# Both SwiGLU stages in written order: transposes by the DMA crossbar, large weight loads in pieces, the forward loop's setup beside the first projection

## The chip, the cores and the metric

The kernel runs on one core of one Trainium2 chip. The metric is the device time of one launch in microseconds (us), the median of several runs. Names used: PE is TensorE (matmuls), DVE VectorE, ACT ScalarE, POOL GpSimd, SP SyncE, which issues transfers and does no arithmetic. A transfer can be issued by SP, ACT or POOL; each is a queue that works in order.

## The reference, cut to what matters

```python
xn = layernorm(x)                      # x: 2048 x 640, bf16
s  = A(xn, mem0, Wq, Wk, Wv, Wo)       # attention over 64 segments of 32 tokens, 8 memory rows handed on
g  = silu(B(xn, w1, w3, w2))           # B: (silu(xn @ w1) * (xn @ w3)) @ w2, inner width 1728
out = x + s * g
# outputs: out, and the gradients of x, mem0, Wq, Wk, Wv, Wo, w1, w3, w2 for a given grad_out
```

A has 32 heads of width 128. Its segments depend on each other only through the 8 memory rows, so the forward pass has a chain of 64 steps, and so has the backward pass. B, the SwiGLU branch, has no such chain: its forward and its backward pass are rows of matmuls.

## The kernel before

The program is a sequence of stages on the one core:

1. `phase1_ln` normalizes 16 tiles of 128 rows, writes the rows (`XN`) and, transposed by PE, the columns (`XNT`) to memory.
2. `phase2_Bfwd` is the SwiGLU forward pass, in four blocks of 512 tokens. For each of 14 chunks of the inner width it forms gate and up product (`pg`, `pu`, lines 1631 and 1634, five matmuls each), the activation `sl` and its gradient factor `ds`, stores both (`SLT`, `DUT`), and keeps the hidden values `hBT`. Then, for each of the four row tiles of the block, it multiplies by w2 (`pz`, 28 matmuls), forms the gate (`GB`), its gradient factor (`DZ`) and the gated gradient (`GS`), and lets PE turn `gs` and `hBT` (lines 1676 and 1683) for storing `GST` and `HB` in the other layout.
3. `phase3_Afwd` begins with the first projection: v, k and q of the first 672 tokens (`b0pb`, line 385), 240 matmuls each. Then it clears its tiles, loads the memory and the first k rows (`kr`), turns them into `kT` (line 562), and runs the forward chain of 64 steps. The "ride" of a step is the part of the inputs of later tokens that is projected along with the memory rows; it is loaded from `XNT`, in the backward chain from `GST`.
4. `phase3b_out` and `phase4_Abwd`: outputs, and the backward chain, whose prologue loads two blocks `gx` (line 763) and the turned WqT.
5. `phase6_Awgrads`, `phase6b_gWo`: the weight gradients of A. `hr`, the rows of the chain's inputs (3 MB), is loaded in it; in the second, `late` loads what B's backward pass needs (`hb_all`, `w2T`).
6. `phase5_Bbwd_ln`: B's backward pass. The gradient `gz` is turned by PE (`gzp`); w2's gradient (`w2a`); then in eight blocks of 256 tokens the gradient at the hidden values (`pghb`, line 1763, 14 chunks of five matmuls), times `du` and `sl` read back (`ggT`, `guT`); the gradient of the rows (`pgxb`, line 1776, 56 matmuls a row tile) with the backward layernorm after it; and PE's turn of `ggT` and `guT` (`ptt`, line 1783) into rows. Last the gradients of w1 and w3 (`wa`, 640 matmuls), the second half from `gutok`, which was stored (`GU`) and is read back.

`turned_load` (line 272) is a transfer that transposes on its way through the DMA crossbar, issued on SP. `k.copy` (lines 90 and 92) is a copy on DVE or ACT. A stage's instructions are put in order by a planner with costs of its own, except where the stage ends with `in_order`, which chains the instructions of every engine in the order in which they are written:

```python
def in_order(k, start):
    ...
    for ins in tc.nc.cur_bb.bb.instructions[start:]:
        p = last.get(ins.engine)
        if p is not None:
            tc.add_manual_dep(ins, p.name, ...)
```

The chains, `phase3b_out` and the weight gradients of A have it. The layernorm, both SwiGLU stages and the first projection don't: the planner orders them, and can put their loads and instructions early, among those of the stage before.

Of the kernel before, what the change touches and what calls it, by code (L numbers as in the profile page):

```python
# [40 lines left out]
class K:  # L41
# [55 lines left out]
    def setup_consts(self):  # L97
# [9 lines left out]
        self.mean_all = const.tile([P, self.NT], F32, name="mean_all")  # L107
# [44 lines left out]
    def setup_dram(self):  # L152
# [7 lines left out]
        self.XNT = mk("XNT", (D, S))  # L160
        self.SLT = mk("SLT", (F, S))
        self.DUT = mk("DUT", (F, S))
        self.HB = mk("HB", (S, F))
# [3 lines left out]
        self.GST = mk("GST", (D, S))  # L167
# [191 lines left out]

def phase3_Afwd(k, W4, Wv, Wk_):  # L360
# [4 lines left out]

    with tc.tile_pool(name="b0", bufs=1) as io, tc.tile_pool(name="b0s", bufs=3) as stp, \
            tc.tile_pool(name="b0p", bufs=4, space=bass.MemoryType.PSUM) as ps:
        xs = io.tile([P, DC, k.NB0], BF16, name="b0x")
        nc.sync.dma_start(xs[:], k.XNT[:, 0:k.NB0].rearrange("(dc p) t -> p dc t", p=P))
        wq = k.A_Wq.rearrange("(dc p) h e -> p dc (h e)", p=P)  # L370
        wo = k.A_Wo.rearrange("h e d -> e h d")
        fetch = [(Wq[:, dc], wq[:, dc]) for dc in range(DC)] + [(Wo[:, h:h + 8], wo[:, h:h + 8]) for h in range(0, H, 8)]
        n = 0
        for wi, (W, dst) in enumerate(((Wv, k.QVX[:, 1]), (Wk_, k.KX[:, :]), (Wq, k.QVX[:, 0]))):
            for x0 in range(0, k.NB0, 112):
                for cg in range(4):
                    if n % 3 == 0 and n > 5 and fetch:
                        nc.scalar.dma_start(*fetch.pop(0))
                    n += 1
                    st = stp.tile([112, 1024], BF16, name="b0st", tag="b0st")  # L380
                    for b in range(2):
                        c0 = cg * 1024 + b * 512
                        pb = ps.tile([112, 512], F32, name="b0pb", tag="b0pb")
                        for dc in range(DC):
                            nc.tensor.matmul(pb[:], xs[:, dc, x0:x0 + 112], W[:, dc, c0:c0 + 512],
                                             start=(dc == 0), stop=(dc == DC - 1))
                        k.copy(st[:, b * 512:(b + 1) * 512], pb[:], eng='vs'[b])
                    nc.sync.dma_start(dst[x0:x0 + 112, cg * 1024:(cg + 1) * 1024], st[:])
        assert not fetch

    with tc.tile_pool(name="ast", bufs=1) as st, tc.tile_pool(name="achain", bufs=1) as ch, \
            tc.tile_pool(name="afill", bufs=1) as fl, \
            tc.tile_pool(name="aps", bufs=1, space=bass.MemoryType.PSUM) as ps, \
            tc.tile_pool(name="apm", bufs=1, space=bass.MemoryType.PSUM) as psm:
# [8 lines left out]
        for i, tt in enumerate(kTs + hxs + qTs + xPs + PTs + [oTm, vt]):  # L403
            (nc.gpsimd, nc.vector)[i % 2].memset(tt[:], 0.0)
        bA, bB, bC = [psm.tile([P, 512], F32, name=f"bank{i}") for i in range(3)]
        pm = bA
        with nc.allow_non_contiguous_dma(reason="tiny mem0 transpose load"):
            for dc in range(DC):
                nc.sync.dma_start(hxs[0][:, dc, 0:8], k.mem0[:, dc * P:(dc + 1) * P].rearrange("m p -> p m"))
            nc.sync.dma_start(k.m_rows(k.HRO, 0), k.mem0)  # L410
# [3 lines left out]
        def ride_ld(t):  # L414
            x0 = k.NB0 + 24 * t
            b, sub = t // 4, t % 4
            if sub == 0 and x0 < S:
                w = min(96, S - x0)
                rt = ch.tile([P, DC, 96], BF16, name="ride", tag="ride")
                nc.sync.dma_start(rt[:, :, 0:w], k.XNT[:, x0:x0 + w].rearrange("(dc p) s -> p dc s", p=P))  # L420
                rides[b] = (rt, w)
# [241 lines left out]
        load_v(0)  # L663
        ride_ld(0)
        ride(0)
        for qd in range(8):
            ld_k(0, qd)
            kprep(0, qd)
# [89 lines left out]
    return Wo  # L758


def gx_ld(k, xs, x0, eng):
    w = min(P, k.S - x0)
    eng.dma_start(xs[:, :, 0:w], k.GST[:, x0:x0 + w].rearrange("(dc p) t -> p dc t", p=P))
# [13 lines left out]
def phase3b_out(k, Wo, W0, W4):  # L777
# [12 lines left out]
    with tc.tile_pool(name="oio", bufs=1) as io, tc.tile_pool(name="oac", bufs=1, space=bass.MemoryType.PSUM) as pa, \  # L790
# [59 lines left out]
        def gox_ld(x0):  # L850
            xs = io.tile([P, DC, P], BF16, name="g0x", tag="g0x", bufs=2)
            gx_ld(k, xs, x0, nc.scalar)
            st["gx", x0] = xs
# [59 lines left out]
def phase4_Abwd(k, out2, WoT, WvT, WkT, WqT, later):  # L913
# [3 lines left out]
    with tc.tile_pool(name="gst", bufs=1) as st, tc.tile_pool(name="gchain", bufs=1) as ch, \  # L917
# [26 lines left out]
        def ride_ld(t):  # L944
# [3 lines left out]
            if sub == 3:  # L948
                rt = ch.tile([P, DC, 96], BF16, name="gride", tag="gride")
                nc.sync.dma_start(rt[:], k.GST[:, 96 * b:96 * b + 96].rearrange("(dc p) s -> p dc s", p=P))  # L950
                rides[b] = rt
# [278 lines left out]
        def gox(x0, cg, b):  # L1230
            if cg == 0 and b == 0:
                uu["gx"] = ch.tile([P, DC, P], BF16, name="gx0", tag="xp", bufs=1)
                gx_ld(k, uu["gx"], x0, nc.gpsimd)
# [31 lines left out]
def phase6_Awgrads(k, X, out0, out3, out4, out5):  # L1265
# [12 lines left out]
    with tc.tile_pool(name="h6i", bufs=3) as io, tc.tile_pool(name="h6", bufs=1) as hp, \  # L1278
# [173 lines left out]
        for qd in range(8):  # L1452
            u0 = NTL * qd
            for p in range(NTL):
# [16 lines left out]
                if u == 6:  # L1471
                    nc.sync.dma_start(hr[0:120], k.HRO[0:120 * NF, :].rearrange("(t p) d -> p t d", p=120))
# [25 lines left out]
def phase6b_gWo(k, gow, orr0, out6, gz, late):  # L1498
# [4 lines left out]
    with tc.tile_pool(name="o6", bufs=1) as hp, tc.tile_pool(name="o6i", bufs=2) as io, \  # L1503
# [28 lines left out]
        for qd in range(8):  # L1532
            orr = orrs[qd]
            for jp in range(2):
# [4 lines left out]
                if qd > 1 and late:  # L1539
                    out_, in_ = late.pop(0)  # L1540
                    if in_ is k.w2:
                        turned_load(k, out_, in_)
                    else:
                        nc.scalar.dma_start(out_, in_)
# [8 lines left out]
                for j in range(2):  # L1553
# [4 lines left out]
                    nc.sync.dma_start(out6f[hh * P:(hh + 1) * P, :], ot[:])  # L1558
# [5 lines left out]
def phase1_ln(k: K):  # L1564
    nc, tc = k.nc, k.tc
    D, DC, NT = k.D, k.DC, k.NT
    with tc.tile_pool(name="ln_io", bufs=3) as io, tc.tile_pool(name="ln_sm", bufs=4) as sm, \
            tc.tile_pool(name="ln_ps", bufs=2, space=bass.MemoryType.PSUM) as ps:
        half = D // 2
        assert half <= nc.vector.BN_STATS_FMAX  # L1570
        for tt in range(NT):
            xt = io.tile([P, D], BF16, name="xt", tag="xt")
            k.dma(xt[:], k.A_x[tt * P:(tt + 1) * P, :])
            stats = sm.tile([P, 2, nc.vector.BN_STATS_DIM], F32, name="stats", tag="stats")
            xv = xt[:].rearrange("p (a b) -> p a b", a=2)
            nc.vector.bn_stats(stats[:, 0, :], xv[:, 0, :])
            nc.vector.bn_stats(stats[:, 1, :], xv[:, 1, :])
            mv = sm.tile([P, nc.vector.BN_AGGR_DIM], F32, name="mv", tag="mv")
            nc.vector.bn_aggr(mv[:], stats[:])
            rs = k.rstd_all[:, tt:tt + 1]  # L1580
            nc.scalar.activation(rs, mv[:, 1:2], ACT.Sqrt, bias=k.eps_t[:], scale=1.0)
            nc.vector.reciprocal(rs, rs)
            nc.vector.tensor_copy(k.mean_all[:, tt:tt + 1], mv[:, 0:1])
            nmr = sm.tile([P, 1], F32, name="nmr", tag="nmr")
            nc.vector.tensor_tensor(nmr[:], mv[:, 0:1], rs, ALU.mult)
            nc.vector.tensor_scalar(nmr[:], nmr[:], -1.0, None, op0=ALU.mult)
            xn = io.tile([P, D], BF16, name="xn_t", tag="xn_t")
            nc.vector.tensor_scalar(xn[:], xt[:], rs, nmr[:], op0=ALU.mult, op1=ALU.add)
# [323 lines left out]
```

## Time and profile before

| | |
|---|---|
| Time, median of 3 runs | 5405.11 us (5395.47 to 5411.18) |
| Span of the profiled run | 5405.4 us |
| PE busy | 4823.1 us, 89% |
| DVE, ACT, POOL busy | 43%, 32%, 29% |
| Mean granted clock of PE | 0.951 |
| First useful matmul (`pg`) | 61.5 us |
| First projection | 327.7 to 489 us |
| First step of the forward chain | 514.4 us |
| B's backward pass, from w2's gradient on | 4933 to 5405 us |

A share of busy time is an average over stages with different limits. The first 514 us and the last 472 us are those that the change rewrites; the stages between are touched in a few loads.

### The profile page before, as it was taken

The page shows a single profiled execution, that of the slowest core. Times are in us where ns is not written, and L with a number is a line of the kernel's source. Part 1 is how long each engine was busy: PE and PEld are TensorE (multiplying, and loading weights), DVE is VectorE, ACT ScalarE, POOL GpSimd, SP SyncE. Part 2 cuts the span into 40 slices and gives each one's busy share as a digit, 9 for nine tenths or more (in the row PEclk, how much of TensorE's full clock was granted, in tenths as well). Part 3 has the DMA queues.
Part 4 walks back from the last instruction along what each step waited for, and adds up shares of the span by engine and source line. Part 5 has one row for each costly group of instructions (what it writes and reads, how often), then busy time and mean ns, then how long its engine had stood idle before and what let it go on. Part 6 is the DMA issues. An engine that isn't in the chain of part 4 may idle for free. (4 is left out here: it accounts for less than half of the span.)

```text
span 5405.4 us, 163107 instructions
## 1 busy us (share of the span) xinstructions
PE 4823.1 (89%) x66012; PEld 3045.0 (56%) x66012; DVE 2298.6 (43%) x7285; ACT 1750.8 (32%) x4913; POOL 1558.0 (29%) x2673
## 2 busy tenths in 40 slices
PE   4988899998999785999999999699999999998999
PEld 2544555555555453655666665555666555666665
DVE  5833555555555423544544443322333222311551
ACT  2422455555555512323333332222233222300111
POOL 0000234334444302333333332523344333310100
PEclk9998999999999786999999999899999999999999
DMA  7553455555554397666766665743555544666332
GB/s 254 175 189 92 128 158 160 153 156 156 160 156 147 116 200 166 177 186 177 196 179 185 181 174 135 165 98 104 126 134 130 115 102 101 170 212 154 122 103 95
DMA packets 1004358, 822.92 MB, mean 152 GB/s; under 512 B 507009, under 2 KB 892333, under 8 KB 1000929
## 3 DMA queue, kind: packets, MB, share of 16 engines
q1 hardware_dynamic: 780562, 579.28, 39.3%
q0 software_dynamic: 95696, 155.10, 10.5%
q10 hardware_dynamic: 127347, 78.10, 5.1%
q8 instruction: 521, 8.54, 0.7%
q14 instruction: 232, 1.90, 0.1%
HBM read 476.95 MB, written 303.09 MB: 144 GB/s over the span
## 5 line engine op out<-in xcount | busy, mean ns | idle before, releaser
L1411 PE MATMUL wg<-gr,hr 128*128 128x512 bf16 x2400 | 529.7, 382 | 16.3 <-DVE dST L1335 13.0
L1390 PE MATMUL g<-w,ghacc 128*128 128x320 bf16 x3072 | 446.4, 303 | 0.0
L1411 PEld LDWEIGHTS <-hr 128*128 128x128 bf16 x2400 | 235.4, 98 | 302.0 <-issue 28.1
L1390 PEld LDWEIGHTS <-ghacc 128*128 128x128 bf16 x3072 | 297.4, 99 | 113.9
L308 PEld LDWEIGHTS <-hx 128*32 128x32 bf16 x7680 | 180.9, 98 | 172.1 <-issue 17.2
L90 DVE CAST wgo<-wg 128x512 bf16<-128x512 f32 x72 | 47.5, 687 | 524.6 <-issue 247.6
L90 DVE CAST stg<-bank 128x512 bf16<-128x512 f32 x256 | 177.0, 691 | 212.0 <-PE bank L308 208.6
L327 PEld LDWEIGHTS <-gkv 128*8 128x8 bf16 x8192 | 190.6, 88 | 108.7 <-DVE gkv L1002 24.3
L611 ACT ACTIVATE xP<-xsp,xnm 120x120 bf16<-120x120 f32 (+1 forms) x704 | 240.0, 375 | 8.7 <-DVE xnm L607 5.4
L660 POOL DMA_DIRECT2D OR<-xv x163 | 92.6, 568 | 473.7 <-ACT xv L659 352.6
L1154 POOL DMA_DIRECT2D DSR<-gdS x176 | 101.1, 575 | 428.5 <-DVE gdS L1152 410.0
L92 ACT CAST wgo<-wg 128x512 bf16<-128x512 f32 x48 | 25.8, 589 | 572.4 <-PE wg L1411 572.4
L1223 PE MATMUL gbank<-WqT,ident 128*128 128x512 bf16 x640 | 203.6, 402 | 0.0
L622 POOL TENSOR_TENSOR xP<-xP,xrz 120x480 bf16<-120x480 bf16 x163 | 161.7, 992 | 136.2 <-ACT xP L611 96.2
L1399 DVE TENSOR_TENSOR ghacc<-ghacc,g 128x320 f32<-128x320 f32 x192 | 93.7, 488 | 236.1 <-PE g L1390 236.1
L1351 ACT CAST gr<-r6p 120x512 bf16<-120x512 f32 x160 | 93.9, 587 | 295.8 <-PE r6p L1344 294.7
L1152 DVE SCALAR_TENSOR_TENSOR gdS<-gdp,Dx,gPr 120x120 bf16<-120x120 f32 (+1 forms) x680 | 182.9, 331 | 0.0
L308 PE MATMUL gbank<-WoT,gox 128*32 128x512 bf16 x2560 | 154.7, 388 | 24.3 <-POOL gox L957 21.0
L1359 POOL DMA_DIRECT2D GSP<-grs x48 | 25.6, 538 | 518.3 <-ACT grs L1351 499.4
L92 ACT COPY ghacc<-t6g 128x768 bf16<-128x768 bf16 (+1 forms) x176 | 137.1, 779 | 106.0 <-PE t6g L1375 102.7
L1123 POOL DMA_DIRECT2D VTD<-gvT x176 | 130.9, 746 | 139.6 <-ACT gvT L1122 116.5
L327 PE MATMUL bank<-Wo,oTm 128*32 128x320 bf16 x4032 | 170.1, 320 | 0.1
(342 smaller groups left out, 11161.0 us busy)
## 6 DMA issues: line engine op xcount, KB each, us to landing
QVS<-stg SPq DMA_DIRECT2D x128, 256.0 KB
gqv<-QVS SPq DMA_DIRECT2D x108, 192.0 KB
vTt<-VTD SPq DMA_DIRECT2D x64, 320.0 KB
VTD<-gvT POOLq DMA_DIRECT2D x168, 120.0 KB, 3.7
DSR<-gdS POOLq DMA_DIRECT2D x168, 120.0 KB, 3.4
dS<-DSR SPq DMA_DIRECT2D x168, 120.0 KB
P<-PR SPq DMA_DIRECT2D x168, 120.0 KB
gPr<-PR SPq DMA_DIRECT2D x164, 120.0 KB
```

Source lines behind the costliest of these rows:

```text
L90: return nc.vector.tensor_copy(out, in_)
L92: return nc.scalar.copy(out, in_)
L308: k.nc.tensor.matmul(bank[32 * g:32 * g + 32, :], x[:, dc, :], W[:, dc, c0:c0 + 512], start=(dc == 0), stop=(dc == k.DC - 1), tile_positio ...
L327: k.nc.tensor.matmul(pm[p0:p0 + nq, 0:320], x[:, h, :], W[:, h, 320 * b:320 * b + 320], start=(first and i == 0), stop=(last and i == 15), ...
L611: nc.scalar.activation(Pb[0:n, j, 0:n], sp[0:n, j, :], ACT.Exp, bias=nmx[0:n, j:j + 1], scale=k.scale, accum_out=Z[0:n, j:j + 1])
L622: eng.tensor_tensor(Pb[0:n, :, 0:n], Pb[0:n, :, 0:n], bc_last(rz[0:n], n), ALU.mult)
L1123: nc.gpsimd.dma_start(k.VTD[tl][:, :, h0:h0 + 4, :], vTq[:])
L1152: nc.vector.scalar_tensor_tensor(dS[0:n, j, 0:n], dp[0:n, j, :], Dx[0:n, j:j + 1], Pr[0:n, j, 0:n], op0=ALU.subtract, op1=ALU.mult)
L1154: nc.gpsimd.dma_start(k.DSR[tl][:, h0:h0 + 4, :], dS[0:n])
L1223: nc.tensor.matmul((bA if g in ("W1", "G1", "G2") else bB)[:], k.ident[:], WqT[:, 0, 0:512], start=True, stop=True)
L1390: nc.tensor.matmul(pg[:], ring[:, i, j, r0:r0 + P], Ws[qd][i][:, j, 320 * h:320 * h + 320], start=(i == 0 and j == 0), stop=(i == 2 and j ...
L1411: nc.tensor.matmul(accs[dc][:], hr[:, tl, dc * P:(dc + 1) * P], grs[i][:, tl, :], start=(tl == 0), stop=(tl == NF - 1))
```

## The change

Both SwiGLU stages are written in software-pipelined order and closed with `in_order`. Layernorm and forward pass become one stage, `phase12_ln_Bfwd`: it loads four row tiles and the first 512 columns of w1 and w3 first, and normalizes the other 12 tiles among the chunks of the first block; the products with w2 of a block run among the chunks of the next. Every transpose by PE in these stages is replaced by `turned_load`, from memory or from one tile on the chip to another; `XNT` and `GST` are no longer kept, and `HB` and `GU` are kept in the layout in which they arise. Stores of these stages move from SP to POOL, w2's and Wo's outputs to POOL and ACT. Wv, Wk and `hr` are loaded in pieces. The projection of v moves to the end of `phase12_ln_Bfwd`, and the setup of the chain (clearing, memory rows, first k) into the projection of k and q.

```diff
+def phase12_ln_Bfwd(k: K, Wv, Wk_):
...
+        def fetch(blk):
+            xnT = io.tile([P, DC, BLK], BF16, name="xnT_b", tag="xnT_b")
+            for i in range(2):
+                turned_load(k, xnT[:, :, i * BLK // 2:(i + 1) * BLK // 2], k.XN[blk * BLK + i * BLK // 2:blk * BLK + (i + 1) * BLK // 2, :])
...
+            nsig = wk.tile([P, BLK], BF16, name="nsig", tag="nsig", bufs=1)
+            nc.scalar.activation(nsig[:fsz], pg[:fsz], ACT.Sigmoid, scale=-1.0)
...
+            ds = wk.tile([P, BLK], BF16, name="ds", tag="ds", bufs=3)
+            nc.vector.tensor_tensor(ds[:fsz], nsig[:fsz], sl[:fsz], ALU.mult)
+            nc.vector.tensor_tensor(ds[:fsz], sig[:fsz], ds[:fsz], ALU.add)
+            nc.gpsimd.dma_start(k.SLT[fc * P:fc * P + fsz, cols], sl[:fsz])
+            nc.gpsimd.tensor_tensor(ds[:fsz], ds[:fsz], ut[:fsz], ALU.mult)
+            nc.gpsimd.dma_start(k.DUT[fc * P:fc * P + fsz, cols], ds[:fsz])
...
+        for tt in range(TB):
+            ln_ld(tt)
+        for w, src in ((w1s, k.w1), (w3s, k.w3)):
+            nc.scalar.dma_start(w[:, :, 0:512], src.rearrange("(dc p) f -> p dc f", p=P)[:, :, 0:512])
...
+        fetch(0)
+        for w, src in ((w1s, k.w1), (w3s, k.w3)):
+            nc.sync.dma_start(w[:, :, 512:F], src.rearrange("(dc p) f -> p dc f", p=P)[:, :, 512:F])
...
+        for blk in range(NBLK):
             for fc in range(FC):
+                hidden(blk, fc)
+                if blk in (1, 2) and fc % 3 == 1:
+                    W, src = ((Wv, k.A_Wv), (Wk_, k.A_Wk))[blk - 1]
+                    nc.scalar.dma_start(W[:, fc // 3, :], ...)
+                if blk == 0:
+                    g, m = fc // 4 + 1, fc % 4
+                    if g < 4:
+                        if m < 2:
+                            ln_stats(TB * g + 2 * m)
+                            ln_stats(TB * g + 2 * m + 1)
+                        else:
+                            if m == 2:
+                                ln_rstd(TB * g, TB * g + TB)
+                            ln_rows(TB * g + 2 * m - 4)
+                            ln_rows(TB * g + 2 * m - 3)
...
+                elif fc < 9 and fc % 2 == 0:
+                    up(blk - 1, fc // 2 - 1)
...
+            first_rows(k, ps, stage, xa, off, Wv, k.QVX[:, 1], x0, cg, tag="pg", w=512)
+        in_order(k, start)
```

```diff
+def first_part(k, Wv, Wk_, Wq, Wo, kTs, vt, hxs, rest):
...
+        for x0 in range(0, k.NB0, 112):
+            turned_load(k, xs[:, :, x0:x0 + 112], k.XN[x0:x0 + 112, :])
...
+        for i, tt in enumerate(kTs + hxs + rest + [vt]):
+            nc.gpsimd.memset(tt[:], 0.0)
...
+                    first_rows(k, ps, lambda: ..., xs, 0, W, dst, x0, cg)
+                    if n >= 26 and n % 2 == 0 and (n - 26) // 2 < 9:
+                        i = (n - 26) // 2
+                        if i > 0:
+                            kturn(i - 1)
+                        if i < 8:
+                            kload(i)
...
-                nc.sync.dma_start(rt[:, :, 0:w], k.XNT[:, x0:x0 + w].rearrange("(dc p) s -> p dc s", p=P))
+                turned_load(k, rt[:, :, 0:w], k.XN[x0:x0 + w, :])
...
-                gx_ld(k, uu["gx"], x0, nc.gpsimd)
+                gx_ld(k, uu["gx"], x0)
...
-                if u == 6:
-                    nc.sync.dma_start(hr[0:120], k.HRO[0:120 * NF, :].rearrange("(t p) d -> p t d", p=120))
+                if 6 <= u < 11:
+                    c = 4 * (u - 6)
+                    nc.sync.dma_start(hr[0:120, c:c + 4], k.HRO[120 * c:120 * c + 480, :].rearrange("(t p) d -> p t d", p=120))
+                if u == 11:
                     nc.sync.dma_start(hr[120:P], k.HRO[120 * NF:k.NR, :].rearrange("(t r) d -> r t d", r=8))
```

In the backward pass of B (`phase5_Bbwd_ln`), `hid` is one chunk pair's gradient at the hidden values and `rowgrad` a generator that hands out the row gradient 16 matmuls at a time between them:

```diff
-        for t0 in range(0, NT, 2):
-            rows = slice(t0 * P, (t0 + 2) * P)
-            late.append((hb[:, t0:t0 + 2, :], k.HB[rows, :].rearrange("(t p) f -> p t f", p=P)))
+        for f in range(0, F, 432):
+            late.append((hb[:, :, f:f + 432], k.HB[f:f + 432, :]))
...
-                        for dc in range(DC):
-                            nc.tensor.transpose(pt[:, dc, :], gz[:, tt, dc * P:(dc + 1) * P], k.ident[:])
-                        k.copy(gzT[:, :, tt * P:(tt + 1) * P], pt[:], eng='vs'[tt % 2])
+                        turned_load(k, gzT[:, :, tt * P:(tt + 1) * P], gz[:, tt, :])
...
+                            nc.vector.tensor_tensor(ggT[0:fsz, fc, :], pg[0:fsz, :], du[0:fsz, c, :], ALU.mult)
+                            nc.vector.tensor_tensor(guT[0:fsz, fc, :], pg[0:fsz, :], sl[0:fsz, c, :], ALU.mult)
+                            turned_load(k, ggtok[:, 2 * b:2 * b + 2, fc * P:fc * P + fsz], ggT[0:fsz, fc, :])
...
+                    for n, (b, i) in enumerate(pairs):
+                        ld(n + 3)
+                        hid(b, i)
+                        if later:
+                            norm2(*later.pop(0))
+                        next(work, None)
+                        if i == FC // 2 - 1:
+                            for _ in work:
+                                pass
+                            hid_out(b)
+                            rows_ld(b)
+                            work = rowgrad(b)
...
+                    in_order(k, start)
...
-                for t0 in range(0, NT, 2):
-                    nc.scalar.dma_start(gutok[:, t0:t0 + 2, :], GU[t0 * P:(t0 + 2) * P, :].rearrange("(t p) f -> p t f", p=P))
+                for f in range(4):
+                    turned_load(k, gutok[:, :, 432 * f:432 * f + 432], GU[432 * f:432 * f + 432, :])
```

## The prediction

> **What bounds the kernel now.** I read the slices of the page first.
>
> ```profile
> PE   4988899998999785999999999699999999998999
> DMA  7553455555554397666766665743555544666332
> ```
>
> A slice is 135 us. TensorE is at 8 or 9 nearly everywhere, so only its idle stretches can be won: the first four slices and the last four hold the stages that the change rewrites, the dips at slices 14 to 16 and 26 lie elsewhere. Next the busy time by stage, at the head. Columns: stretch, its length, busy us (instructions) of PE, PEld, DVE, ACT, POOL, granted clock, DMA share, GB/s.
>
> ```profile
> 0.00:20.00 20.00, 0.00 (x0) 0.00 (x0) 1.48 (x9) 0.00 (x0) 3.33 (x22) 1.00 0.93 339
> 20.00:61.50 41.50, 11.04 (x80) 7.46 (x81) 31.63 (x136) 11.30 (x25) 0.00 (x0) 1.00 0.78 216
> 61.50:123.00 61.50, 38.14 (x140) 15.34 (x139) 28.81 (x62) 16.50 (x28) 3.12 (x4) 0.81 0.70 270
> ...
> 437.30:490.00 52.70, 52.00 (x241) 31.09 (x239) 16.58 (x24) 14.62 (x25) 0.00 (x0) 1.00 0.34 107
> 490.00:520.00 30.00, 9.12 (x100) 4.56 (x100) 4.51 (x9) 3.61 (x8) 7.58 (x9) 0.60 0.30 54
> ```
>
> Three holes: 61.5 us before the first useful matmul, with the DMA engines nearly full of weights; the first SwiGLU block at 38 of 61.5; and the 30 us between the projections (last matmul 489) and the forward chain (first step 514.4). The waits of PE up to 520 us name them (us in total, times, longest):
>
> ```profile
> PE lnT L1592 <- DVE nmr L1585: 24.3, 1, 24.3
> PE pg L1631 <- DVE sl L1639: 23.3, 3, 10.3
> PE kpt L562 <- DMA kr<-KX: 21.6, 4, 14.7
> PE lnT L1592 <- DVE xn_t L1588: 18.8, 9, 4.4
> ```
>
> DVE's `sl` itself waits for the store of the old `sl` ("11.81 <-DMA SLT<-sl" in the timeline of DVE), so hole two is a DMA queue too. Then the tail.
>
> ```profile
> 4933.00:5021.00 88.00, 73.58 (x528) 47.33 (x528) 10.06 (x23) 9.73 (x20) 1.43 (x2) 0.92 0.47 93
> 5021.00:5054.00 33.00, 28.67 (x211) 19.50 (x211) 15.39 (x39) 3.10 (x6) 7.05 (x9) 0.95 0.56 177
> 5054.00:5282.00 228.00, 211.69 (x1696) 144.54 (x1694) 130.66 (x315) 40.16 (x60) 19.55 (x14) 0.99 0.35 108
> ```
>
> PE is near full there, so the chain of waits must say with what. Its pieces are start, length, what:
>
> ```profile
> 4943.62 18.06 DMA x<-in_B_w_dram
> ...
> 5027.58 8.45 DMA sl<-SLT
> ```
>
> Of the rest PE's own transposes are what goes: the timeline has 14 `ptt` transposes in about 0.97 us. The price of the crossbar transposes that replace them is in the view of line 272 (duration min/median/max of the issue on SP, first and last start):
>
> ```profile
> L272 SPq DMA_TRANSPOSE w<-in_A_Wv_dram x8: 2519/2560/2757, 3408.4 to 4521.5; - x8
> ...
> L272 SPq DMA_TRANSPOSE x<-in_B_w_dram x4: 1210/4874/15805, 4932.7 to 4959.5; - x4
> L272 SPq DMA_TRANSPOSE w2T<-in_B_w_dram x1: 19622/19622/19622, 4891.9 to 4891.9; - x1
> ```
>
> A 640x128 piece occupies SP 1.2 us, a 640x512 piece 2.56: about 0.8 fixed and 0.43 per 640x128. `w2T` (2.21 MB) took 19.6 with 2.56 MB of `orr` ahead of it, which at the 339 GB/s of the first slice is 7.5: 12 us, some 180 GB/s.
>
> Two places in the middle are touched as well (PE and SP timelines):
>
> ```profile
> 3486.15 0.58 PE L1334 MATMUL t<-ident,dS 120*128 120x120 bf16 x4 [16.57 <-DMA dS<-DSR]
> ```
>
> ```profile
> 3461.35 6.36 SPq L1473 DMA_DIRECT2D hr<-HRO  x1
> ```
>
> PE idles 16.6 us just after the 3 MB `hr` load.
>
> **What the Trainium skill says.** "DMA: Bandwidth & Descriptors", section "DMA Transpose (X-bar)": the plain transpose is issued from SP or ACT only, and two such streams must not be in flight together. The trace has all of them on SP; so will the new kernel, and its stores have to leave SP. The same page, "Latency and other measured facts", gives 261 GB/s for one kernel's transposes; the trace shows about 180, which I use. "SBUF — State Buffer", "Who interferes with whom": a DVE instruction with two SBUF inputs and a GpSimd instruction that reads SBUF block each other. No row of before isolates that. "ScalarE: Activation LUTs", "Table sets: the hidden batching unit": sqrt and sigmoid are in different sets. Agreed: a table load of 1.28 us stands before each of the two uses here.
>
> **The head, part by part.**
> Start. Only four row tiles (0.65 MB) and 512 columns of w1, w3 (1.3 MB) come first: 2 MB at the 339 GB/s of the first slice is 6 us. Statistics of four tiles at 1.1 us, rstd, four normalizations at 0.44: 13. The last store of XN is taken at 3 us (POOL stores land in 2.4 to 3.7), and two transposes of 256 rows, beside the 2.2 MB of w2, at 3 each: first matmul at 22 (18 to 28). The rest of w1 and w3, 3.1 MB, lands near 31, about when the first four column chunks (4 x 2.16) have run: no wait.
> Block 0. PE needs 14 x 10 x 0.216 = 30. DVE needs per chunk 0.60 + 3 x 0.35 = 1.7 (distances of the starts of `sl` and of the 0.42 us products; the 0.68 `scalar_tensor_tensor` goes, one product goes to POOL), 24 for 14, and 12 tiles of layernorm at 1.4 are 17: 41. Three sqrt calls among sigmoids bring six table loads, 7.7 us on ACT, of which DVE feels most: 48 (32 to 55).
> Blocks 1 to 3. PE: 30.2, and four times 28 matmuls of the up product in 4.28, 17.1: 47.3 each, 142 together. DVE is at 24 + 4 x 2.2 = 33, ACT 14 x 1.8 + 6 = 31, below PE. POOL: two issues of 0.57 and a 512-wide product, from the 480-wide `xP` product of 0.997 us taken as 1.06: 2.2 a chunk, 31, and 12 stores of 0.57: 38. So nothing but PE, unless the shared port stretches POOL's product.
> Last up products 17 and the v projection 24 x 2 x 1.08 = 52, with evictions queued behind the up product's DVE chain, 1 us each time: 74. k and q: 103.7 (51.8 in each window of before), 2 for the turning of k, which hides its loads, 3 for the first crossbar load of `xs`: 109. Memsets (POOL), `hx`, `vt` and `kT` lie beside this. Handover 3.
> Sum 22 + 48 + 142 + 74 + 109 + 3 = 398, against 514: **116 us won**. Removed PE transposes (16 x 2 x 0.6) are in it.
>
> **The middle.** `hb` arrives turned in four pieces of 1.77 MB (9 us of DMA each) beside 2.56 MB of `orr` (7.5), loads and stores (5) in 22 us of PE: just fits, and `orr` is asked for a whole 22 us ahead. `hr` in pieces, 0.6 MB between the loads of a unit: 0 to 16 off, I take 8. The first `gx` load in the backward prologue moves from POOL to SP behind a 6.6 us transpose of WqT that PE then waits for: 8 on; the second came after 17.9 us of waiting already and doesn't change. Rides turned by DMA (28 times about 1 us of SP instead of 0.4): behind them wait only dumps and loads for later steps. Zero in sum.
>
> **The tail.** w2's gradient: 448 x 0.151 = 67, three changes of accumulators 1 each: 70 from 4933, since the w1T, w3T loads (24 us of SP) and 16 crossbar turns of `gz` (1.2 to 1.9 each, 30 at most) end before: 5003. Hidden gradient: 112 x 0.545 = 61, row gradient 896 x 0.151 = 135; together 196, where before took 261. Start and first block, on DVE (14 x 0.84 against 7.7): 6. SP turns 112 tiles 128x256. SBUF to SBUF is not in the trace; from 0.8 fixed + 0.17 it is 1.0, and with the fixed part doubled 1.8; I take 1.2: 134 us beside 196 of PE. DVE: 94 + 16 x 3.1 = 144, below. Then `wa`, 640 x 0.181 = 116, last stores 5, 4 for changes. The four turned loads of `gutok`, 7.1 MB at 180 GB/s = 39 us, lie under the first 58 of `wa`. 70 + 6 + 196 + 116 + 9 = 397 from 4933, against 472: **75 won**.
>
> Total: 5405 - 116 - 75 = 5214.
>
> **Rivals.**
> POOL sets the head. Stores of both blocks now go through it, and its product may be blocked by DVE, which is two-input work 70% of the time. At 3.1 us a chunk, 56 chunks are 174, the 12 XN and 48 row stores 34: head 25 longer, and slower-landing stores 10: 5250. For: POOL at 38 of 47. Against: `xP`, also beside DVE, is 0.98 to 1.00 in every run.
> The crossbar sets the tail. With a turn from SBUF at 2.5 us, 112 are 280 against 196 of PE: 84 more, 5298. For: no row from SBUF. Against: the fixed part seen is 0.8.
> It ends slower. If turns from SBUF cost 4.5 us (504 us for 112, 72 for gz), the tail is 310 longer than forecast: 5524. For: nothing but the gap in the trace. A milder one, turned `hb` and `gutok` late by 20, is 5234 and inside the range.
>
> **How the numbers follow.** Forecast and its near variants 0.72, POOL 0.14, crossbar 0.09, slower 0.04; 0.01 for no change. Time 5214. Low: start at 18, block 0 on PE (32), `hr` 16, no `gx` loss: 4 + 16 + 8 + 8 = 36 less, 5178; I say 5170. High: POOL's 5250 with `gutok` late by 20 and 10 more at the start: 5280. Above lies the crossbar case and the slower one, 13 in 100. Faster 0.95, same 0.01, slower 0.04.
>
> **What would show it.** First `pg` matmul near 22; first chain step (Wk with hx) near 398; in block 0 PE waits for DVE, in blocks 1 to 3 it doesn't; no wait on `kr` at the start of the chain; POOL product near 1.06; DMA_TRANSPOSE of ggtok near 1.2 on SP; w2a ends near 5003 minus the shift of 116, and `wa` starts about 204 later without idle. Wrong if PE waits in the tail for `ggtok`, `gzT` or `gutok`, or if POOL is above 90% in the head.

## The result, and the profile after

The changed kernel takes 5322.24 us (5321.22 to 5325.9, 4 runs) against 5406.31 for the kernel before in the same comparison: ratio 0.9848, 95% interval 0.9831 to 0.9865. It is faster by 84 us, where 191 were forecast, and its time lies above the forecast range. The tail came as forecast, the head won a quarter of what it was to win, and the middle lost instead of staying even.

The slices of the page, of the kernel after (a slice is 133 us):

```profile
PE   6878899999999784989999999789999999999999
DMA  7753455555554497676766676555553455449783
```

The last four slices of PE are now full, where the first of them stood at 8 before; the first five are not. The same stretches in the windows view of the kernel after: block 1, 2 and 3 of the SwiGLU forward pass, the v projection, a hole, the k and the q projection. Columns as before: stretch, length, busy us (instructions) of PE, PEld, DVE, ACT, POOL, granted clock, DMA share, GB/s.

```profile
79.10:146.10 67.00, 54.29 (x252) 26.51 (x251) 38.43 (x74) 27.49 (x50) 40.96 (x59) 0.87 0.81 236
146.10:203.60 57.50, 48.97 (x254) 25.35 (x254) 36.49 (x71) 27.13 (x50) 39.34 (x56) 0.94 0.84 240
203.60:262.40 58.80, 49.62 (x252) 25.30 (x252) 36.43 (x73) 27.15 (x51) 40.09 (x57) 0.94 0.64 165
262.40:342.00 79.60, 71.68 (x352) 43.42 (x352) 28.46 (x47) 20.09 (x34) 13.80 (x22) 0.96 0.43 132
342.00:351.00 9.00, 0.15 (x1) 0.18 (x2) 0.00 (x0) 0.59 (x1) 8.94 (x9) 0.79 0.62 180
351.00:432.30 81.30, 60.02 (x241) 33.95 (x240) 15.94 (x24) 13.48 (x23) 9.09 (x12) 0.90 0.66 190
432.30:485.70 53.40, 53.40 (x273) 32.18 (x272) 19.46 (x32) 14.07 (x24) 0.00 (x0) 1.00 0.39 124
```

No engine is full in the three blocks: PE is busy 54, 49 and 50 us of 67, 58 and 59, DVE, ACT and POOL less. So they stand for each other. The waits from 15 to 490 us, kernel after (us in total, times, longest):

```profile
ACT nsig L1668 <- DVE ds L1675: 61.4, 39, 11.1
DVE b0st L90 <- DMA KX<-b0st: 53.3, 11, 9.3
...
ACT dz L1703 <- DVE gb L1700: 49.6, 16, 9.6
PE pg L1663 <- DVE sl L1672: 47.5, 26, 5.9
...
DVE sl L1672 <- DMA SLT<-sl: 28.9, 7, 6.1
...
PE b0pb L366 <- DVE b0st L90: 26.5, 12, 5.4
```

PE waits for DVE, DVE for stores, and ACT for DVE. The timeline of the kernel after in block 1, for DVE, ACT and PE, shows how one of these stands runs through the engines (start, duration, instruction, idle before it and what ended it):

```profile
93.69 0.69 DVE L1672 TENSOR_TENSOR sl<-pg,sig 128x512 bf16<-128x512 f32 x1 [5.43 <-DMA SLT<-sl]
...
98.85 0.43 DVE L1675 TENSOR_TENSOR ds<-nsig,sl 128x512 bf16<-128x512 bf16 x1 [3.94 <-DMA DUT<-ds]
...
99.65 0.82 DVE L1700 TENSOR_TENSOR gb<-pz,sz 128x640 bf16<-128x640 f32 x1
...
104.19 0.69 DVE L1672 TENSOR_TENSOR sl<-pg,sig 128x512 bf16<-128x512 f32 x1 [1.53 <-ACT nsig L1668]
```

```profile
100.50 0.70 ACT L1703 ACTIVATE dz<-pz 128x640 bf16<-128x640 f32 x1 [9.59 <-DVE gb L1700]
...
103.07 0.60 ACT L1666 ACTIVATE sig<-pg 128x512 bf16<-128x512 f32 x1 [1.87 <-DVE gs L1708]
```

```profile
90.01 1.24 PE L1663 MATMUL pg<-xnT_b,w1s 128*128 128x512 bf16 x5
91.09 1.24 PE L1663 MATMUL pu<-xnT_b,w3s 128*128 128x512 bf16 x5
94.43 2.22 PE L1663 MATMUL pg<-xnT_b,w1s 128*128 128x512 bf16 x5 [2.10 <-DVE sl L1672]
...
104.93 2.29 PE L1663 MATMUL pg<-xnT_b,w1s 128*128 128x512 bf16 x5 [2.69 <-DVE sl L1672]
```

DVE stands 5.4 us for the store of an old `sl` to free its buffer; PE waits 2.1 for the new `sl`. Then DVE stands 3.9 more for a store of `ds`. `gb` is behind it on DVE, ACT's `dz` waits 9.6 for `gb`, the sigmoids of the next chunk (`sig` at 103.07) stand behind `dz` on ACT, the next `sl` (104.19) comes after them, and PE has waited again, for 2.7. When PE goes on, five matmuls take 2.22 and 2.29 us instead of 1.24.

The tail of the kernel after, by tiles (duration min/median/max, first and last start), in two views, of `ggtok` and of `w2a`:

```profile
L1971 PE MATMUL wa<-ggtok,xn_all x320: 343/346/346, 5200.3 to 5258.5; 128*128 128x432 bf16 x160
L269 SPq DMA_TRANSPOSE ggtok<-ggT x112: 1167/1197/3194, 5000.1 to 5184.7; - x112
```

```profile
L1827 PE MATMUL w2a<-gz_all,hb_all x448: 296/299/323, 4931.0 to 4997.7; 128*128 128x320 bf16 x139, 128*64 128x320 bf16 x11
```

From 4931.0 to 5324.2 are 393.2 us, against 471.7 before: 78.5 won.

### The profile page after: what moved, and what is told of

It reads as the page before. It is cut to its first block, busy times and chain, and to the rows that moved or that the text cites. A ratio compares the mean times of both kernels' runs of the same rounds, so it can differ in the third digit from the quotient of the medians.

```text
span 5324.2 us, 161443 instructions
## 1 busy us (share of the span) xinstructions
PE 4746.0 (89%) x65100; PEld 3002.1 (56%) x65100; DVE 2241.8 (42%) x7110; ACT 1725.8 (32%) x4891; POOL 1824.6 (34%) x3069
## 5 line engine op out<-in xcount | busy, mean ns | idle before, releaser
L1165 POOL DMA_DIRECT2D VTD<-gvT x176 | 130.1, 741 | 155.7 <-ACT gvT L1164 122.7
L336 DVE TENSOR_TENSOR fsum<-gbank,fup 64x160 bf16<-64x160 f32 x128 | 40.5, 316 | 316.0 <-ACT fup L335 316.0
L534 DVE COPY vt<-stg 8x512 bf16<-8x512 bf16 x512 | 162.5, 317 | 20.5 <-ACT stg L92 12.9
```

The source lines that it names most:

```text
L534: nc.vector.tensor_copy(vt[p0:p0 + 8, c0:c0 + 512], sv[32 * g:32 * g + 8, b * 512:(b + 1) * 512])
L1165: nc.gpsimd.dma_start(k.VTD[tl][:, :, h0:h0 + 4, :], vTq[:])
```

## The experiments

Times of single stages are read from the profiles, one profiled execution each, since the two chains, which no edit here touches unless said, differ by up to 20 us from run to run (shown below). No single edit brings the total clear of the changed kernel's interval on the fast side (e14 only just misses), so what each won is read from its stage. "Hidden stretch" is the time from the first `pg` to the first product of the v projection: 238.5 in the kernel after. Four more kernels with the same code in it (e2, e3, e7, e8) took 245.0, 246.0, 242.0 and 252.1, so that the mean of five is 244.7.

**e1: a second buffer for `nsig`.**

```diff
-            nsig = wk.tile([P, BLK], BF16, name="nsig", tag="nsig", bufs=1)
+            nsig = wk.tile([P, BLK], BF16, name="nsig", tag="nsig", bufs=2)
```

> The kernel after, with two buffers for nsig instead of one. Theory (a loop through that one buffer: the next nsig waits for ds, sl waits for nsig because both read the same PSUM bank, ds waits for sl): the hidden blocks, first pg at 23.9 to first product of Wv at 262, shrink from 238 to about 212; the chain starts near 460 instead of 485.7, the time is near 5297. Rival (the stores of sl and ds, slowed by the weight traffic, set these blocks): under 5 us off. Second rival (POOL's product and DVE block each other): under 10 us off.

5325.25 us, ratio 0.9858 (0.9835 to 0.988); hidden stretch 235.2. The loop isn't what holds blocks 1 and 2 (69.2 and 60.5). Block 3 alone came out shorter, 50.5 where the five kernels above took 58.3 to 60.2.

**e2: the pieces of Wq and Wo at half the rate.**

```diff
-                    if n % 2 == 0 and fetch:
+                    if n % 4 == 0 and fetch:
```

> The kernel after, with the pieces of Wq and Wo asked for every fourth turn instead of every second. Theory (the k projection waits because its stores stand behind 10 MB of weights): its 81 us fall to about 62, the time by about 20 to 5302. Rival (two stage buffers are too few at any pace, stores take 6 us or more from 1 KB rows alone): under 6 us off. It may also turn out late: Wq's last piece is asked for 8 turns before it is used, some 17 us; if it lands late the q projection grows from 53.

5322.04 us, ratio 0.9851 (0.9831 to 0.9871). k fell from 81.4 to 72.4, q rose from 53.4 to 63.4: nothing won.

**e3: the two `gx` loads ahead of the other loads of the prologue**, each into a tile of its own.

```diff
-                uu["gx"] = ch.tile([P, DC, P], BF16, name="gx0", tag="xp", bufs=1)
-                gx_ld(k, uu["gx"], x0)
+                uu["gx"] = gxs.pop(0)
...
+        gxs = []
+        for x0 in range(k.GB0, k.GB0 + k.GL, P)[::-1]:
+            gxs.append(ch.tile([P, DC, P], BF16, name="gx0", tag=("xp", "vTt")[len(gxs)], bufs=1))
+            gx_ld(k, gxs[-1], x0)
         for _ in range(6):
             ld_next()
```

> The kernel after, with both gx loads of the backward prologue asked for ahead of its other loads and of WqT, each into a tile of its own. Theory (the prologue lost 14 us because PE waits 12.9 and 20.8 us for gx behind crossbar loads of WqT on SP): from the first gdp to the first chain step, 129.8 in the kernel after and 115.7 in the kernel before, falls to about 100, the time by about 30 to 5292. Rival (the crossbar loads of WqT, 4 of 12 us, and the quarter loads behind them on SP bound this stretch): 115 or more, at most 14 off.

5317.12 us, ratio 0.9843 (0.9825 to 0.9861). From the first `gdp` to the first chain step 115.5, where the kernel after took 129.8 and the kernel before 115.7. In the kernel after the tile view of `gx` has PE waiting twice for these loads:

```profile
PE gbank L813: 33.7, 2
```

In the kernel before the list of waits has two as well:

```profile
PE gbank L771 <- DMA gx<-GST: 23.7, 2, 17.9
```

No such line is in e3, yet 14 us came off, not 34: as the rival said, what stands behind WqT's four transposes (6.5 to 12.1 us of SP each in e3) is the next limit. There ACT stands three times, 12.7 to 14.6 us each, for the store of an old `gks`, which SP issues just after such a transpose, and PE waits 18.1 us in all for ACT. With the two loads early, the loss of 14 is gone.

**e4: the kernel before with the backward rides turned by the crossbar.**

```diff
-                nc.sync.dma_start(rt[:], k.GST[:, 96 * b:96 * b + 96].rearrange("(dc p) s -> p dc s", p=P))
+                turned_load(k, rt[:], k.GS[96 * b:96 * b + 96, :])
```

> The kernel before, with only the rides of the backward chain turned from GS by the crossbar. Theory (the backward chain lost 18 us because each of these loads now holds SP and the DMA engines for a transpose): first to last step, 1251.0 in the kernel before, becomes about 1269, the time 5423. Rival (the extra time comes from where the copies of rows fall beside the steps, or from other parts of the change): within 5 us of the kernel before.

5425.25 us, ratio 1.0028 (1.0002 to 1.0054). First to last step 1270.9 us against 1251.0. The issue on SP, in the kernel before and in e4:

```profile
L950 SPq DMA_DIRECT2D gride<-GST x14: 387/395/723, 2130.4 to 3154.0; - x14
```

```profile
L272 SPq DMA_TRANSPOSE gride<-GS x14: 1251/1266/2066, 2135.9 to 3181.2; - x14
```

With this one edit the backward chain is as long in its profile as in the kernel after (1269.5); how much of that is the spread of single runs is worked out below.

**e5: the stores of HB on SP's queue instead of POOL's** (`nc.gpsimd` becomes `nc.sync` in both stores of `hidden_out`).

> The kernel after, with the 1.7 MB stores of HB issued on SP's queue instead of POOL's. Theory Q (the small stores of sl, ds, gb, dz and gs stand in POOL's queue behind HB, which takes 22 us to land in block 1; DVE waits for their buffers, ACT and PE wait for DVE): from first pg to the first product of Wv, 238.5 in the kernel after and 235 to 246 in three others with this code, becomes about 215, and the longest landing of a store of sl falls from 18.9 to under 8 us. Rival (the DMA engines are shared whatever the queue; it is the sum of the traffic): within 8 us of 240. Rival A (ACT, held in order by waits for DVE): also within 8 us.

5326.79 us, ratio 0.9877 (0.985 to 0.9905); hidden stretch 243.8, longest landing of `sl` 21.7. So it is not the order within POOL's queue.

**e6: ACT no longer stands for DVE.**

```diff
-            gb = wk.tile([P, D], BF16, name="gb", tag="gb")
-            nc.vector.tensor_tensor(halves(gb), pz[:, :, 0:320], halves(sz), ALU.mult)
-            nc.gpsimd.dma_start(k.GB[rows, :], gb[:])
             dz = wk.tile([P, D], BF16, name="dz", tag="dz")
             nc.scalar.activation(halves(dz), pz[:, :, 0:320], ACT.Sigmoid, scale=-1.0)
+            gb = wk.tile([P, D], BF16, name="gb", tag="gb")
+            nc.vector.tensor_tensor(halves(gb), pz[:, :, 0:320], halves(sz), ALU.mult)
+            nc.gpsimd.dma_start(k.GB[rows, :], gb[:])
```

and, beside it, `bufs=2` for `nsig` and `bufs=3` for `Gt`.

> The kernel after, with the three places changed at which ACT, which works in order, stands for DVE: dz's sigmoid written before gb, two nsig buffers, three Gt buffers. Theory A (ACT stood 49.6 us for gb before dz, 61.4 for ds before nsig, 12 more for Gt; the sigmoids of the next chunk are behind it): from first pg to Wv 210 to 215 instead of 240. Rival Q (stores behind HB): the stands move to DVE's waits for stores of sl and ds, and the stretch stays within 8 us of 240.

5301.91 us, ratio 0.9828 (0.9805 to 0.985); hidden stretch 221.5. Blocks 1 to 3 in the windows view:

```profile
79.30:141.90 62.60, 50.23 (x247) 25.65 (x252) 40.04 (x72) 26.63 (x49) 40.02 (x58) 0.89 0.79 250
141.90:196.10 54.20, 48.07 (x247) 25.19 (x252) 39.81 (x72) 26.96 (x51) 39.99 (x57) 0.97 0.81 256
196.10:245.30 49.20, 46.27 (x248) 24.62 (x253) 42.39 (x73) 27.25 (x52) 40.31 (x57) 1.00 0.62 197
```

The gain is more than any rival allowed and less than theory A: something else is left in blocks 1 and 2.

**e7: three stage buffers in the k and q projections** (`tc.tile_pool(name="b0s", bufs=3)`; the change had gone from 3 to 2).

> The kernel after, with three stage buffers in the k and q projections instead of two. Theory (two buffers leave one store's landing of some 9 us no cover; the kernel before has three): the k projection, 81 us, becomes about 62, q stays 53. Rival (pieces of Wq and Wo starve the stores at any number of buffers): over 72. In the run with the pieces at half the rate k took 72.4 and q 63.4.

5308.56 us, ratio 0.9836 (0.98 to 0.9873). k 61.7, q 53.4: as the theory said, 20 of k's 29 us over the forecast. PE's wait for DVE's evictions in k, 21.3 us in the kernel after, is now 6.2.

**e8: the backward ride's turned load issued by ACT** (`nc.scalar.dma_start_transpose`).

> The kernel after, with the turned load of the ride in the backward chain issued by ACT instead of SP. Theory S (what costs 18 to 20 us is SP's time: 1.27 us instead of 0.40 for each of 14 loads, with SP's loads of gqv behind them already late): first to last step 1251 instead of 1269.5 (1259 to 1264 in three other runs of this code). Rival D (the transpose itself costs, in the DMA engines): 1259 to 1270 as now. Rival (ACT is as full as SP there): above 1270.

5357.18 us, ratio 0.9928 (0.9906 to 0.995); first to last step 1279.7. Moving the issue to ACT makes it worse, so it doesn't tell whether SP's time or the transpose costs.

**e9: e6, e7 and e3 together.**

> The kernel after with the three edits at ACT, three stage buffers and the early gx loads together. If the three gains lie in different stages and add (20 in the hidden blocks, 20 in the k projection, 14 in the backward prologue): 54 under the kernel after, 5268. If a later stage gives one back, as the chains did by up to 14 us from run to run: 5282 or more.

5273.38 us, ratio 0.9749 (0.9719 to 0.978); hidden stretch 221.6, as in e6. The gains add; the chain starts at 442.3 instead of 485.7, and in the profiled run the forward chain gave 20 back (1329.6 against 1309.4).

**e10: the kernel of e9 with the traffic moved**: the last lines stand in the loop of the v projection.

```diff
-                if blk in (1, 2) and fc % 3 == 1:
-                    W, src = ((Wv, k.A_Wv), (Wk_, k.A_Wk))[blk - 1]
-                    nc.scalar.dma_start(W[:, fc // 3, :], src.rearrange("(dc p) h e -> p dc (h e)", p=P)[:, fc // 3, :])
+        WVAT = [(2, 1), (2, 6), (2, 11), (3, 5), (3, 9)]
...
+                if (blk, fc) in WVAT:
+                    dc = WVAT.index((blk, fc))
+                    nc.scalar.dma_start(Wv[:, dc, :], k.A_Wv.rearrange("(dc p) h e -> p dc (h e)", p=P)[:, dc, :])
+                if (blk, fc) == (3, 1):
+                    k.x_rows(k.HRO, k.XN, nc.sync)
...
-                    if fc == 13:
-                        k.x_rows(k.HRO, k.XN, nc.sync)
...
+            if n % 3 == 0 and n < 15:
+                nc.scalar.dma_start(Wk_[:, n // 3, :], k.A_Wk.rearrange("(dc p) h e -> p dc (h e)", p=P)[:, n // 3, :])
```

> The kernel of e9, and in it Wv's pieces go to blocks 2 and 3, Wk's into the v projection, the copy of XN into HRO from block 1 into block 3. Theory T (what is left in blocks 1 and 2 is traffic: HB, HRO and a weight at once; block 3 of e6, with none, took 49.2 against 47.3 of PE): block 1 falls from 62.6 to 52, block 2 stays near 54, block 3 rises from 49 to at most 54; first pg to Wv from 221 to about 212, and the time is 9 under e9. Rival (blocks 1 and 2 are long for another reason, such as POOL's product or two sig buffers): block 1 over 59, first pg to Wv within 4 of 221.

5272.98 us, ratio 0.9752 (0.9716 to 0.9787); hidden stretch 209.2. Its three blocks in the windows view:

```profile
78.90:125.60 46.70, 46.03 (x252) 24.66 (x252) 43.69 (x72) 26.30 (x49) 39.98 (x58) 1.00 0.58 189
125.60:184.90 59.30, 47.97 (x252) 25.00 (x252) 42.32 (x72) 27.11 (x51) 40.09 (x57) 0.91 0.67 237
184.90:232.80 47.90, 46.19 (x252) 24.57 (x251) 42.45 (x72) 27.23 (x52) 40.06 (x57) 1.00 0.78 231
```

Block 1 went from 62.6 in e6 to 46.7, PE being busy for 46.0 of it. The DMA view of block 1 shows what changed (issues: KB each, median us to landing), first the kernel after, then e10:

```profile
HB<-hBT POOLq DMA_DIRECT2D x1, 1664.0 KB, 22.1
...
GS<-gs POOLq DMA_DIRECT2D x4, 160.0 KB, 10.4
```

```profile
HB<-hBT POOLq DMA_DIRECT2D x1, 1664.0 KB, 9.1
...
GS<-gs POOLq DMA_DIRECT2D x4, 160.0 KB, 2.2
```

Block 2 got longer, 59.3 against 54.2 in e6. The edit did not put the copy into HRO where its text puts it: the timelines of SP, DVE and PE have it in block 2.

```profile
128.47 0.99 SPq L250 DMA_DIRECT2D HRO<-XN  x1
```

```profile
141.58 0.42 DVE L1678 TENSOR_TENSOR ds<-nsig,sl 128x512 bf16<-128x512 bf16 x1 [6.99 <-DMA DUT<-ds]
...
147.43 0.69 DVE L1675 TENSOR_TENSOR sl<-pg,sig 128x512 bf16<-128x512 f32 x1 [4.96 <-DMA SLT<-sl]
```

```profile
148.17 2.29 PE L1666 MATMUL pg<-xnT_b,w1s 128*128 128x512 bf16 x5 [9.09 <-DVE sl L1675]
```

The copy is written in block 3, but all that SP had ahead of it was the load of that block's columns, which went out as block 1 ended. So copy, a piece of Wv (130.6) and HB (135.2) started within 7 us, two stores landed late, and PE stood 9.1 us, most of what it was idle in that block (11.4). It was the same in e14 and e15 (copy at 130.1 and 129.0, block 2 61.4 and 59.6). Block 2 got longer though its pieces of weights fell from five to three, so the copy counts; how much of block 1's gain is the copy's and how much Wv's no run separates. The total time did not follow the 12 us of the hidden stretch within what this comparison can tell.

**e11: the kernel before, with SP busy for longer at each ride.**

```diff
+                for i in range(2):
+                    nc.sync.dma_start(spare[2 * b + i], k.GS[96 * b + i, :])
```

> The kernel before, with two more small copies (1.3 KB each, DRAM to DRAM, read by nobody) issued on SP behind each ride load of the backward chain: about 0.8 us more of SP each time, as much as the transpose takes more, and no transpose. Theory S (SP's time is what the turned rides cost): first to last step from 1251.0 to 1262 to 1271. Rival D (the transpose itself): 1248 to 1254.

5417.51 us, ratio 1.0029 (1.0017 to 1.0041); first to last step 1264.6, 13.6 more than in the kernel before. The two copies held SP 0.58 us each at the median, 1.2 a ride where the transpose takes 0.9 more than the plain load. So SP's time alone, without a transpose, costs; what it costs at exactly the transpose's 0.9 was not run.

**e12: the kernel before with `hr` in pieces** (the edit of the change, alone).

> The kernel before, with hr loaded in five pieces between a unit's loads, as in the kernel after. From the first t to the first wg 127.5 becomes about 118 (the kernel after has 118.1), the time 9 less. Rival (that gain came from elsewhere in the change): 126 or more. Its backward chain is the kernel before's: if that is 1251 again within 3, then the 18.5 us by which the kernel after exceeds it are more than chance; if it is 1258 or more, part of them is.

5405.3 us, ratio 0.9991 (0.9976 to 1.0006). First `t` to first `wg` 122.7, between theory and rival: 5 us from the pieces, not 9 (e4 and e11, with the one load, took 127.4 and 125.8). The backward chain was 1252.5, the forward chain 1323.0 against 1313.2 in the kernel before, with the same code.

**e13: only the order of `dz` and `gb`**, as in e6.

> The kernel after, with dz's sigmoid written before gb and nothing else. If this is the one of e6's three edits that counts (nsig's second buffer alone gave 3 to 11 us): first pg to Wv 222 to 228, where the kernel after and four others with this code took 238 to 252. If the three only work together: 236 or more.

5317.8 us, ratio 0.9834 (0.9809 to 0.9859); hidden stretch 241.0: alone it wins nothing.

**e14: only the traffic moved**, as in e10.

> The kernel after, with the traffic moved as in e10 and ACT's order as it was. If ACT's stands are only how late stores reach PE: first pg to Wv near 210, as in e10. If the two causes are separate and add (ACT about 20, traffic 12): 226 to 230. If ACT's order hides the gain of the traffic: 236 or more.

5294.85 us, ratio 0.9804 (0.9777 to 0.9832); hidden stretch 215.7. Between the first two theories: 29 off the mean of 244.7, where freeing ACT took 23 and both together took 36 (e10; e15 repeats it with 209.6). So the two are for the most part one chain, late stores that reach PE through an engine that works in order; each link cut alone wins most of it.

**e15: e10 with the pieces of Wq and Wo every third turn.**

> The kernel of e10, with the pieces of Wq and Wo every third turn instead of every second. Theory (with three stage buffers, what the k projection has left over 52 is this traffic): k falls from 62.3 to 56, q stays at 53.5; the time 6 under e10. Rival (no more to be had, or q waits for its last piece): k and q together over 113.

5252.38 us, ratio 0.9724 (0.9704 to 0.9745), the lowest here. k 58.3 and q 57.5, together 115.8 as in e10: the rival's case, so the edit itself won nothing there, and in the two profiled runs the lower time goes with chains that ran shorter (forward 1312.9 against 1326.2, backward 1255.1 against 1261.2). What the runs show is that e9, e10 and e15, with the edits of e3, e6 and e7 in them, all beat the changed kernel, with intervals that do not touch its own.

## Why the prediction was wrong, step by step

The head was to take 398 us up to the first chain step and took 485.7 (all in us).

| Step | forecast | measured | over |
|---|---|---|---|
| start | 22 | 23.9 | 2 |
| block 0 | 48 | 55.2 | 7 |
| blocks 1 to 3 | 142 | 183.3 | 41 |
| last up products and v | 74 | 79.6 | 6 |
| first load of `xs` | 3 | 8.9 | 6 |
| k | 52 | 81.4 | 29 |
| q and `kT` | 54 | 53.4 | -1 |
| handover | 3 | 0 | -3 |

**The step that failed is "So nothing but PE" for blocks 1 to 3.** It compared the engines' sums (PE 47.3, POOL 38, DVE 33, ACT 31 a block) and took the largest for the time. The sums were about right: PE 46 in e10, POOL 40, ACT 27, DVE 36 to 44. What it left out was the traffic that the change puts into the same 60 us, Wv or Wk, HB and the copy into HRO, and the finite buffers of `sl` and `ds` behind which every engine stands in order when a store lands late. The forecast priced those stores by issue alone, though it had itself read a wait of 11.81 us for the store of an old `sl` in the first block of the kernel before. Of the 183.3 us, PE was busy 152.9 and idle 30.4. In e10 it was busy 140.2 and idle 13.7. So of the 29.4 us between them 16.7 is idle time and 12.7 are the same matmuls run at a lower granted clock: 0.87 in block 1 of the kernel after, 1.00 in e10. With the two causes taken out, block 1 and block 3 take 46.7 and 47.9 against the forecast 47.3: the price of the matmuls was right. Block 2 took 59.3 in e10, with copy, weight and HB all in it, as the trace above shows; no run here takes the copy out of the blocks altogether.

**The second is "k and q: 103.7".** It took the projections' rate from the kernel before, where the 10 MB of Wq and Wo come in beside v (57.8 us), and didn't see that the change asks for them from k's first turn on and cuts the stage buffers from three to two. The third buffer alone brings 20 of the 29 back (e7). Of the rest, some 9 us, e7 has 6.2 as PE's wait for DVE's evictions and the remainder as matmuls at a lower clock (0.95). It goes with the pieces: when they are spread over more turns, q takes longer (e2, e15). In e2 PE waits in q 6.2 us for DVE, and no wait for a weight is in view.

**The middle was "zero in sum" and lost 26**: prologue 14 lost, backward chain 18.5, `hr` 9 won, 3 for the rest. The `gx` waits were nearly as forecast: the first rose from 5.8 to 12.9, 7 where 8 was forecast, the second, which "doesn't change", from 17.9 to 20.8. The other 4 of the prologue's 14 are open; e3 takes out the whole loss. **The third step that failed is the rides**, put at nothing because "behind them wait only dumps and loads for later steps". In twelve profiles of kernels with turned rides on SP and the code of the change, the chain took 1254.6 to 1273.6, mean 1261.0, against 1251.0 and 1252.5 in two with plain rides. So some 9 us of the 18.5 is the rides' and the rest is the spread of single runs. PE's idle time in the chain says much the same: 91.3 us in the kernel after against 79.4 and 81.7 in the two. Some 7 of the 18.5 is busy time of the same number of matmuls. That more of SP's time is enough to lengthen the chain is shown (e11); that the transpose itself costs nothing more is not.

**`hr` in pieces** was to bring 8; the stretch gained 9.4 in the kernel after, and the edit alone 5.

**The tail was right**: 393.2 us against a forecast 397, 75 won against 78.5. `ggtok`'s turn, with no row to go by, was a guess between 1.0 and 1.8; 1.2 was taken, and the median is 1.197, which is luck. The tail did not hang on it: 112 turns of 1.2 us stand beside 201.5 us. PE waits for none of `ggtok`, `gzT` and `gutok`; it waits 9.9 us in all for DVE's `guT`. w2's gradient took 67.8, forecast 70; from its end to the first `wa` 201.5, forecast about 204.

**The rivals.** The crossbar did not set the tail. POOL did not set the head (the 25 us put on it don't follow from the rival's own figures: 174 + 34 against 48 + 142 is 18): its product took 1.16 us against 1.06, it was busy 61% to 68% of blocks 1 to 3, and in e10 block 1 ran at PE's rate with POOL's work unchanged. Late DMA was in the list for the tail, at 20 us, and for the head only as "slower-landing stores 10" within POOL's case; as a case of its own it was missing. The 7 us over in block 0 and the 6 each at v and `xs` are measured and not taken apart.

## What to carry to other kernels

Before a stage is put down as bound by its fullest engine, add up its DMA bytes and ask how many buffers each store leaves behind it: as an estimate from these figures, three buffers of a 2.2 us chunk cover a landing of some 4 us, two chunks, and not one of 10. When a diff shortens a stage, the transfers put beside it need a place too; weights and copies with slack belong where the DMA share is low (here the v projection, at 0.43). Where a transfer starts is set by what stands ahead of it on the engine that issues it, not by the loop in which it is written: see the copy in e10. On an engine that works in order, write what needs no other engine ahead of what does, and compare the buffer counts on both sides of a diff line by line.

## What the runs showed of the hardware beyond the forecast

A short wait of PE can cost twice. After 2.1 us of idle time five matmuls took 2.22 us where five took 1.24 before it; the granted clock was 1.00 in the 16 us up to the wait's end and 0.56 in the 3.9 us after it. The Trainium skill, "TensorE: Matmul & The Clock Gate", section "Part 1: The HAM clock gate", says that the clock is halved after an idle window of about 3.4 us and needs a busy one to come back. The near halving agrees; here a gap of 2.1 us was followed by it.

The granted clock also makes the chains unsteady, with no gap of PE in view. The same step of the forward chain, in the same code, in the kernel before and in e12 (PE timeline):

```profile
806.11 2.34 PE L308 MATMUL bank<-Wk,hx 128*32 128x512 bf16 x40
```

```profile
805.79 3.99 PE L308 MATMUL bank<-Wk,hx 128*32 128x512 bf16 x40
```

The granted clock in 806 to 810 us was 1.00 in the first and 0.60 in the second. Over 17 profiles the forward chain took 1309 to 1330 us, and in the pair above, with the same code, it is PE's busy time that differs and not its idle time: 1190.7 and 122.5 in the kernel before, 1202.9 and 120.1 in e12. That is why a gain of 12 us in the head can't be seen in a single total.

A product of POOL can hold up one of DVE. In the kernel after a product of DVE on two tiles from SBUF took 1.47 us when POOL's product (1.17 us) started at the same moment, and 0.42 without:

```profile
171.24 0.42 DVE L1673 TENSOR_TENSOR hBT<-sl,ut 128x512 bf16<-128x512 bf16 x1
...
174.22 1.47 DVE L1673 TENSOR_TENSOR hBT<-sl,ut 128x512 bf16<-128x512 bf16 x1
```

The Trainium skill, "SBUF — State Buffer", section "Who interferes with whom", says that a DVE instruction with two SBUF inputs contends with a GpSimd instruction that reads SBUF; the trace agrees on DVE's side, and POOL's product stayed at 1.14 to 1.17. In block 1 of e10 this product of DVE took 0.83 on average against 0.61 in the kernel after, DVE was busy 44 of 46.7 us, and still PE was the bound there.
